# A decode block's second MLP layer with batches on partitions in four column groups, gate and residual as two VectorE operations, and one store of 32 rows

## The chip, the cores and the metric

One core of a Trainium2 chip (trn2). The metric is the device time of one execution in microseconds (us). The *span* of an execution, from its first to its last instruction, is 1.7 to 2.1 us shorter than the device time. A *landing* is the moment when the last part of a transfer has reported its arrival; the *issue* of a transfer is the instruction on SyncE or ScalarE that starts it; a *piece* is one contiguous run of bytes in it.

## The reference

A decode step of one transformer block for 8 sequences: modulation vectors from `silu(c) @ w_mod`, a layer norm, attention of 32 heads over a cache of 8192 keys and values, and an MLP. What the change touches is the last line:

```python
h = _layernorm(x) * (1 + cb) + sb
x = x + gb * (relu(h @ w1 + b1) ** 2 @ w2 + b2)     # x: 8 x 1 x 512; w1: 512 x 1792; w2: 1792 x 512
```

`gb` is a different gate for each batch and each column. Almost all the work of the kernel is elsewhere: the two caches are 268 MB.

## The kernel before

The kernel is written engine by engine with explicit semaphores: `op(engine, instruction, [what it waits for])`. A list of waits may hold both an operation and a transfer. Activations are kept transposed (128 columns of the model on the partitions, batches along the free side), so W2 is the stationary operand, 128x128 at a time, and eight batches move past it. At the end four matmuls with an identity turn the gated result back to batches on partitions, and the residual is accumulated there by four more:

```python
d_w2 = [dma("sync", s_w2[i], ...W2v[:, a:z, :]... B_w2[128*a:128*z]...)          # four pieces of W2
        for i, (a, z, j) in enumerate(((0, 4, 4), (4, 8, 4), (8, 12, 4), (12, 14, 2)))]
... # attention output, residual x1T, layer norm, first layer -> hidT (two halves, tokens k_sq[0], k_sq[1])
for f in range(FT):                                                              # FT = 14
    for k in range(KT):                                                          # KT = 4
        t = matmul(yT_ps[:, k, :], W2v[:, f, k*128:(k+1)*128], hidT[:, f, :]),   # waits [k_sq[f // 8], d_w2[f // 4]]
... # four matmuls put x1T into o_ps
k_y2 = op("vector", tensor_tensor(y2T, yT_ps, mod(5), mult), [t])
for cc in (1, 0):
    ... # two matmuls each add y2T.T to o_ps[64*cc : 64*cc+8, :]
    ... # ScalarE (cc = 1) or VectorE (cc = 0) copies these 8 rows to out_sb
    d_o.append(dma(("sync", "scalar")[cc], s_out[cc], outf[:, 256*cc:256*(cc+1)] <- out_sb[rows, :]))
Pg.wait("sync", d_o)
```

(`matmul(...)` and `tensor_tensor(...)` stand for the calls on the engine; "..." marks the rest.)

Of the kernel before, what the change touches and what calls it, by code (L numbers as in the profile page):

```python
# [5 lines left out]
ACT = mybir.ActivationFunctionType  # L6
ALU = mybir.AluOpType
AX = mybir.AxisListType
FP32 = mybir.dt.float32
BF16 = mybir.dt.bfloat16  # L10
# [23 lines left out]
class Prog:  # L34
# [19 lines left out]
    def op(self, eng, fn, deps=()):  # L54
        o = Op(eng, fn, deps, None, self.at)
        o.tok = Tok(o, self.at)
        self.ops[eng].append(o)
        return o.tok

    def dma(self, eng, sem, fn, deps=()):  # L60
        self.dma_n[sem] = self.dma_n.get(sem, 0) + 16
        self.ops[eng].append(Op(eng, fn, deps, sem, self.at))
        return Tok(None, self.at, sem, self.dma_n[sem])
# [105 lines left out]
def bass_adaLN_cond__gqa_block_cached__dense_activation_squared_relu__decode_kernel(  # L169
    nc, A_x, A_k_cache, A_v_cache, A_wq, A_wo, B_x, B_w1, B_b1, B_w2, B_b2, c, w_mod, out):  # L170
    B, _, D = A_x.shape
# [5 lines left out]
    KT = D // 128  # L177
    FT = F // 128
# [8 lines left out]
    with ExitStack() as es:  # L187
        E = es.enter_context
        sb = lambda name, shape, dt: E(nc.sbuf_tensor(name, shape, dt))
# [18 lines left out]
        IDENT = sb("IDENT", [128, 128], BF16)  # L208
# [4 lines left out]
        SEL = sb("SEL", [128, 4, 8], BF16)  # L213
# [9 lines left out]
        xT = sb("xT", [128, KT, B], BF16)  # L223
        modT = sb("modT", [128, 24, B], FP32)
        cb1 = sb("cb1", [128, KT, B], FP32)
        b_row = sb("b_row", [4, 512 + 128], BF16)
        SELB = sb("SELB", [4, 4, B], BF16)
        SELP = sb("SELP", [128, B], FP32)
        x1T = sb("x1T", [128, KT, B], BF16)
        sqs = sb("sqs", [128, B], FP32)  # L230
        std2 = sb("std2", [128, B], FP32)
        rstd2 = sb("rstd2", [128, B], FP32)
        hbT = sb("hbT", [128, KT, 2, B], BF16)

        KF = KTb[:, :, :, :].rearrange("p a t r -> p (a t r)")
        c_sb = KF[0:B, 0:512]
# [4 lines left out]
        csT = KF[:, 4096:4096 + 32 * KT].rearrange("p (k r) -> p k r", k=KT)  # L241
        haT = KF[:, 4224:4224 + 32 * KT].rearrange("p (k r) -> p k r", k=KT)
        ca1 = KF[:, 4352:4416].bitcast(FP32).rearrange("p (k b) -> p k b", k=KT)
        tmpT = KF[:, 4416:4480].bitcast(FP32).rearrange("p (k b) -> p k b", k=KT)
        EYE = KF[:, 4480:4544].bitcast(FP32).rearrange("p (g b) -> p g b", g=4)
        EYEB = KF[:, 4544:4576].rearrange("p (g b) -> p g b", g=4)
# [4 lines left out]
        sqT = KF[:, 2432:2496].bitcast(FP32).rearrange("p (k b) -> p k b", k=KT)  # L251
        hidT = KF[:, 2560:2560 + FT * B].rearrange("p (f b) -> p f b", f=FT)
        out_sb = KF[:, 2048:2304]
        oPe = KF[:, 2816:3008].rearrange("p (x j b) -> p x j b", x=6, j=4)
        oP = KF[:, 3008:3072].rearrange("p (g j b) -> p g j b", g=2, j=4)
        proj = KF[:, 4096:5120].bitcast(FP32)
        b1_row, b2_row = b_row[:, 0:512], b_row[:, 512:640]
        y2T = KF[:, 0:KT * B].rearrange("p (k b) -> p k b", k=KT)
        rT = KF[:, 1024:1024 + 2 * FT * B].bitcast(FP32).rearrange("p (f b) -> p f b", f=FT)
# [21 lines left out]
        s_last = [sem(f"d_l{i}") for i in range(3)]  # L281
        s_out = [sem(f"d_o{i}") for i in range(2)]

# [9 lines left out]
        def pool(fn, deps=()):  # L293
            return op("gpsimd", fn, deps)
# [3 lines left out]
        pool(lambda e: e.memset(ONESMB[:], 1.0 / D))  # L298
        pool(lambda e: e.memset(epst[:], EPS))
        pool(lambda e: e.memset(R4[:], 0.0))  # L300
        pool(lambda e: e.memset(Qmask[:], 1.0))
# [8 lines left out]
        def select(ap, pattern, base, cm, fill, cmp, dep):  # L310
            return pool(lambda e: e.affine_select(ap, ap, pattern=pattern, compare_op=cmp, fill=fill,
                                                  base=base, channel_multiplier=cm), [dep])
# [7 lines left out]
        t = pool(lambda e: e.memset(EYEB[:], 0.0))  # L320
        t = select(EYE[:], [[-32, 4], [-1, B]], 0, 1, 1.0, NE, t)
        t = k_eye = select(EYEB[:], [[-32, 4], [-1, B]], 0, 1, 1.0, NE, t)
        k_q0 = pool(lambda e: e.memset(QTm[:], 0.0))
# [8 lines left out]

        for i in range(4):
            for cg in range(4):
                for half in range(2):
                    t = select(SEL[:, i, 4 * half:4 * half + 4], [[-1, 4]], -(32 * cg + 8 * i + 4 * half), 1,
                               1.0, NE, t)

# [3 lines left out]
        t = select(PERM[:], [[-1, 4], [0, 4], [-4, 32]], 0, 1, 1.0, NE, t)  # L342
        t = select(SELB[:], [[-1, 4], [0, B]], 0, 1, 1.0, NE, t)
        t = pool(lambda e: e.memset(oTn[:], 0.0), [t])
# [31 lines left out]
        for k in range(KT):  # L376
            t = op("tensor", lambda e, k=k: e.matmul(csT_ps[:, k, :], cs_k[:, k, :], IDENT[0:B, 0:B],
                                                    is_transpose=True), [k_cs, k_id])
        k_csT = op("vector", lambda e: e.tensor_copy(csT[:, :, 0:B], csT_ps), [t, k_eye])

# [41 lines left out]
        t = op("vector", lambda e: e.tensor_tensor(tmpT[:], hnT_ps, ca1[:], ALU.mult), [t, k_hnT])  # L422
        k_haT = op("vector", lambda e: e.tensor_tensor(haT[:, :, 0:B], tmpT[:], mod(0), ALU.add), [t])
        for i in range(KT):
# [23 lines left out]
        k_sb = op("vector", lambda e: e.tensor_copy(hbT[:, :, 1, :], mod(3)), [k_modT])  # L448
        k_cb1 = op("vector", lambda e: e.tensor_scalar(cb1[:], mod(4), 1.0, None, ALU.add))

        stg_free = [k_modT, None, None, k_QTm]
# [64 lines left out]
        hT_ps = [bank(i)[:, 0:16 * n].rearrange("p (f a b) -> p f a b", f=n, a=2) for i, n in enumerate((8, FT - 8))]  # L516
        yT_ps = bank(2)[:, 0:KT * B].rearrange("p (k b) -> p k b", k=KT)

# [30 lines left out]
        for b in range(B):  # L549
# [76 lines left out]
            for p in range(NP):  # L626
# [47 lines left out]
                else:  # L674
# [29 lines left out]
                    for hh, (f0, n, a, z) in enumerate(((0, 4, 0, 2), (0, 4, 2, 3), (4, 2, 3, 4))):  # L704
                        for j in range(n):
                            op("tensor", lambda e, hh=min(hh, 1), f0=f0 + j, j=j, n=n, a=a, z=z: e.matmul(
                                hT_ps[hh][:, f0:f0 + 4 * (z - a - 1) + 1:4, 1, :], brow(j, n), SELB[:, a:z, :],
                                start=(f0 == 0), stop=False, skip_group_check=True), [d_bb, s_bank_free[min(hh, 1)]])
                    op("tensor", lambda e: e.matmul(
                        yT_ps, b2_row, SELB[:, :, :], start=True, stop=False, skip_group_check=True),  # L710
                        [s_bank_free[2]])
# [24 lines left out]
        t = op("vector", lambda e: e.tensor_tensor(t1T[:], attn_ps, mod(2), ALU.mult), [k_attn])  # L736
        k_x1 = op("vector", lambda e: e.tensor_tensor(x1T[:], t1T[:], xT[:], ALU.add), [t])
        mean_ps = bank(3)[:, 0:B]
# [3 lines left out]
        bc = lambda ap: ap.unsqueeze(1).to_broadcast([128, KT, B])  # L742
        t = op("vector", lambda e: e.tensor_tensor(xcT[:], x1T[:], bc(mean_ps), ALU.subtract), [t])
        k_xc = t
# [7 lines left out]
        for k in range(KT):  # L752
# [4 lines left out]
            for f in range(FT):  # L757
# [3 lines left out]
                if k == KT - 1 and f in (7, FT - 1):  # L761
# [7 lines left out]
                        hidT[:, fs, :], rT[:, fs, :], 0.0, rT[:, fs, :], ALU.max, ALU.mult), [t]))  # L769
        o_ps = bank(4)[:, 0:256]  # L770
        for f in range(FT):
            for k in range(KT):
                t = op("tensor", lambda e, f=f, k=k: e.matmul(  # L773
                    yT_ps[:, k, :], W2v[:, f, k * 128:(k + 1) * 128], hidT[:, f, :],
                    start=False, stop=(f == FT - 1), skip_group_check=True), [k_sq[f // 8], d_w2[f // 4]])
        for cc in range(2):
            for k in range(2):
                op("tensor", lambda e, k=k, cc=cc: e.matmul(
                    o_ps[64 * cc:64 * cc + B, 128 * k:128 * (k + 1)], x1T[:, 2 * cc + k, :], IDENT[:, :],
                    start=(k == 0), stop=False, tile_position=(0, 64 * cc), skip_group_check=True), [k_x1])  # L780
        k_y2 = op("vector", lambda e: e.tensor_tensor(y2T, yT_ps, mod(5), ALU.mult), [t])
        outf = out.rearrange("b s d -> (b s) d")
        d_o = []
        for cc in (1, 0):
            for k in range(2):
                t = op("tensor", lambda e, k=k, cc=cc: e.matmul(
                    o_ps[64 * cc:64 * cc + B, 128 * k:128 * (k + 1)], y2T[:, 2 * cc + k, :], IDENT[:, :],
                    start=False, stop=(k == 1), tile_position=(0, 64 * cc), skip_group_check=True), [k_y2])
            rows = slice(64 * cc, 64 * cc + B)
            if cc == 0:  # L790
                t = op("vector", lambda e, rows=rows: e.tensor_copy(out_sb[rows, :], o_ps[rows, :]), [t])
            else:
                t = op("scalar", lambda e, rows=rows: e.activation(out_sb[rows, :], o_ps[rows, :], ACT.Copy), [t])
            d_o.append(dma(("sync", "scalar")[cc], s_out[cc], lambda e, cc=cc, rows=rows: e.dma_start(
                outf[:, 256 * cc:256 * (cc + 1)], out_sb[rows, :]), [t]))
        Pg.wait("sync", d_o)

# [30 lines left out]
```

## Time and profile before

| | before |
|---|---|
| time, first three runs | 668.56 us median, 668.41 to 669.83 |
| span of the trace | 666.73 us |
| bytes read | 283.66 MB, at 425 GB/s over the span |
| last piece of W2 landed (semaphore in the trace) | 663.33 us |
| last store issued | 664.92 us |

How to read it: the kernel is a stream of bytes with computation beneath it, and only what comes behind the last landing is bare. The prediction shows the lines. I call the stretch from the last W2 landing to the end of the span *the tail*: 666.73 - 663.33 = 3.40 us. The tail, and not the device time, is the measure for this change, since the device time of one and the same kernel moves by more than a microsecond from run to run.

### The profile page before, as it was taken

To read this page: it belongs to the slowest core of one execution; us is meant where nothing else is said; L and a number is where in the kernel's file an instruction comes from. 1 tells how busy PE (TensorE), PEld (TensorE's weight loads), DVE (VectorE), ACT (ScalarE), POOL (GpSimd) and SP (SyncE) were. 2 spreads that over 40 slices of the span, in tenths; PEclk is the share of its full clock that TensorE was granted. 3 is DMA by queue.
4 is the path that set the end of the run, shared out by engine and by line. 5 is a ranking of instruction groups with operands and counts; after the bars stand their busy time and mean duration, and the time that the engine had idled before them with its cause. 6 is when DMAs were issued, how large, how long until landed. Compare 5 with 4: busy or idle time off the path is not lost.

```text
span 666.7 us, 15924 instructions
## 1 busy us (share of the span) xinstructions
PE 528.3 (79%) x7259; PEld 352.2 (53%) x7259; DVE 307.9 (46%) x587; ACT 264.3 (40%) x307; POOL 20.5 (3%) x79
## 2 busy tenths in 40 slices
PE   3494976898849987599858988499776998589887
PEld 2383732675328742477316753287424773277535
DVE  1262741466316652367415662167513673146633
ACT  2151631466115651166314661166512663146611
POOL 7400000000000000000000000000000000000000
PEclk9696998799969999699998999799997999879996
DMA  9999999999999999999999999999999999999997
GB/s 375 437 406 441 419 433 433 425 434 431 438 427 433 433 434 427 434 434 425 434 431 438 427 431 434 434 427 431 438 425 434 433 436 427 431 434 434 427 420 285
DMA packets 12189, 283.85 MB, mean 426 GB/s; under 512 B 1261, under 2 KB 1297, under 8 KB 3601
## 3 DMA queue, kind: packets, MB, share of 16 engines
q1 hardware_dynamic: 12128, 283.65, 99.3%
q8 instruction: 9, 0.15, 0.1%
q10 hardware_dynamic: 48, 0.02, 0.0%
q14 instruction: 4, 0.02, 0.0%
HBM read 283.66 MB, written 0.01 MB: 425 GB/s over the span
## 4 chain that ended last, share of the span: by engine, by line
PE 52%; DMA 38%; ACT 6%; DVE 2%; issue 1%; SPq 0%; DVEq 0%
PE PS L488 36%; DMA ring<-in_A_k_cache_dram 33%; PE PS L505 9%; ACT P_sb L582 5%; DMA ring<-in_A_v_cache_dram 4%; DMA ring<-in_A_wq_dram 2%; PE PS L636 2%; PE PS L478 1%; ACT KTb L493 1%; DVE O_sb L656 1%; PE PS L472 1%; PE PS L594 1%; DVE Pm L608 0%; PE PS L614 0%; PE PS L773 0%
## 5 line engine op out<-in xcount | busy, mean ns | idle before, releaser
L488 PE MATMUL PS<-IDENT,ring 128*128 128x128 bf16 x4096 | 267.1, 227 | 56.2 <-DMA ring<-in_A_k_cache_dram 56.2
L488 PEld LDWEIGHTS PS<-IDENT,ring 128*128 128x128 bf16 x4096 | 246.5, 102 | 104.8 <-DMA ring<-in_A_k_cache_dram 57.4
L493 ACT ACTIVATE KTb<-PS 128x1024 bf16<-128x1024 bf16 x192 | 196.5, 1024 | 236.6 <-PE PS L488 236.6
L495 DVE COPY KTb<-PS 128x1024 bf16<-128x1024 bf16 x320 | 210.0, 688 | 146.5 <-PE PS L488 144.4
L636 PE MATMUL PS<-ring,Pm 128*32 128x512 bf16 x1018 | 67.2, 409 | 24.8 <-DMA ring<-in_A_v_cache_dram 23.9
L505 PE MATMUL PS<-KTb,Qb 128*32 128x512 bf16 x1024 | 79.0, 385 | 4.5 <-ACT KTb L493 4.5
L656 DVE CAST O_sb<-PS 128x512 bf16<-128x512 f32 x31 | 21.5, 692 | 112.7 <-PE PS L636 112.7
L636 PEld LDWEIGHTS PS<-ring,Pm 128*32 128x32 bf16 x1018 | 26.5, 101 | 61.8 <-DMA ring<-in_A_v_cache_dram 33.7
L535 ACT ACTIVATE KTb<-PS 32x192 bf16<-32x192 f32 (+1 forms) x18 | 5.6, 310 | 110.0 <-PE PS L472 103.9
L582 ACT ACTIVATE P_sb<-PS,negm 128x1024 bf16<-128x1024 f32 x32 | 35.2, 1111 | 20.2 <-DVE negm L577 20.2
L478 PE MATMUL PS<-ONES 128*128 128x512 f32 x80 | 42.1, 630 | 0.0
L472 PE MATMUL PS<-IDENT 128*128 128x512 bf16 x112 | 33.4, 380 | 0.0
L594 PE MATMUL PS<-IDENT,P_sb 128*128 128x128 bf16 x256 | 19.9, 220 | 15.4 <-ACT P_sb L582 15.4
L608 DVE COPY Pm<-PS 64x512 bf16<-64x512 bf16 x48 | 20.2, 421 | 25.0 <-PE PS L594 24.5
L594 PEld LDWEIGHTS PS<-IDENT,P_sb 128*128 128x128 bf16 x256 | 14.4, 98 | 25.1 <-ACT P_sb L582 25.1
L505 PEld LDWEIGHTS PS<-KTb,Qb 128*32 128x32 bf16 x1024 | 15.4, 94 | 21.0 <-ACT KTb L493 8.5
L512 DVE TENSOR_REDUCE m<-PS 128x1 f32<-128x512 f32 x32 | 22.1, 689 | 6.6 <-PE PS L505 6.6
L660 PEld LDWEIGHTS PS<-SEL,O_sb 128*128 128x128 bf16 x124 | 5.8, 97 | 30.0 <-DVE O_sb L656 30.0
L478 PEld LDWEIGHTS PS<-ONES 128*128 128x128 f32 x80 | 12.7, 190 | 10.6 <-issue 10.6
L660 PE MATMUL PS<-SEL,O_sb 128*128 128x8 bf16 x124 | 7.8, 169 | 12.3 <-DVE O_sb L656 12.0
L472 PEld LDWEIGHTS PS<-IDENT 128*128 128x128 bf16 x112 | 9.9, 104 | 10.1 <-issue 7.2
L543 PE MATMUL PS<-wo_sb,KTb 128*32 128x512 bf16 x192 | 11.8, 380 | 3.3 <-ACT KTb L535 3.3
(134 smaller groups left out, 147.0 us busy)
## 6 DMA issues: line engine op xcount, KB each, us to landing
ring<-in_A_k_cache_dram SPq DMA_DIRECT2D x32, 4096.0 KB, 34.0
ring<-in_A_v_cache_dram SPq DMA_DIRECT2D x31, 4096.0 KB, 27.8
ring<-in_A_wq_dram SPq DMA_DIRECT2D x1, 4096.0 KB, 19.8
wo_sb<-in_A_wo_dram SPq DMA_DIRECT2D x1, 4096.0 KB, 47.3
ring<-in_w_mod_dram SPq DMA_DIRECT2D x1, 3072.0 KB, 10.5
ring<-in_A_v_cache_dram SPq DMA_DIRECT2D x1, 2048.0 KB, 22.5
ring<-in_B_w_dram SPq DMA_DIRECT2D x3, 512.0 KB, 19.2
ring<-in_B_w_dram SPq DMA_DIRECT2D x1, 1344.0 KB, 17.8
```

The lines of the kernel that those rows point to most:

```text
L472: ts = [op("tensor", lambda e: e.matmul(bank(at).rearrange("p (a r) -> p a r", a=4), IDENT[:, :], rhs)) for _ in range(n)]
L478: ts = [op("tensor", lambda e: e.matmul(bank(at).rearrange("p (a r) -> p a r", a=4), ONES[:, :], rhs)) for _ in range(n)]
L488: t = op("tensor", lambda e, j=j, i=i: e.matmul(STG[j][:, i, :], src[:, 32 * k + 8 * j + i, :], IDENT[:, :], is_transpose=True), [loaded[n ...
L493: stg_free[j] = op("scalar", lambda e, j=j, dst=dst: e.activation(dst, STG[j], ACT.Copy), [t])
L495: stg_free[j] = op("vector", lambda e, j=j, dst=dst: e.tensor_copy(dst, STG[j]), [t])
L505: t = op("tensor", lambda e, hf=hf, q=q, rhs=rhs: e.matmul(PS[32 * q:32 * (q + 1), k, :], Qb[:, 2 * p + hf, :], rhs, start=(p == 0 and hf ...
L512: return op("vector", lambda e: e.tensor_reduce(m4[:, k:k + 1], bank(k), AX.X, ALU.max), [t])
L582: exps.append(op("scalar", lambda e, k=k: e.activation(P_sb[:, k, :, :, :], bank(k).rearrange("p (i x) -> p i x", i=8).unsqueeze(2).to_bro ...
L594: t = op("tensor", lambda e, k=k, i=i: e.matmul(STG[k][:, i, :], P_sb[:, k, i, :, :].rearrange("p h x -> p (h x)"), IDENT[:, :], is_transp ...
L608: done.append(op("vector", lambda e, dst=dst, frm=frm: e.tensor_copy(dst, frm), [t, k_pm]))
L636: t = op("tensor", lambda e, m=m, cg=cg, p=p, vt=vt, Obank=Obank: e.matmul(Obank[32 * cg:32 * (cg + 1), :], lhs[:, p, 32 * m:32 * m + 32], ...
L656: t = op("vector", lambda e, osb=osb, Obank=Obank: e.tensor_copy(osb, Obank), [t])
```

## The change

The intent: make the activations the stationary operand, so that the second layer's result comes out with batches on partitions straight away. The four blocks of 128 output columns go to four column groups of the PE array (output partitions 32k to 32k+31). The closing transposes and copies fall away; gate and residual become two VectorE operations of 128x128, and one store writes 32 rows of 256 B. A column group is 32 wide and there are eight batches, so the activations are padded: batch b sits in column 4b, with zeros between. The output row of batch b in block k is then on partition 32k + 4b, that is on every fourth partition. The core of the diff:

```diff
-        SELB = sb("SELB", [4, 4, B], BF16)
+        SELB = sb("SELB", [4, 4, 32], BF16)
-        x1T = sb("x1T", [128, KT, B], BF16)
+        x1w = sb("x1w", [128, KT, B, 4], BF16)
+        hidw = sb("hidw", [128, FT, B, 4], BF16)
+        mod5 = sb("mod5", [128, 128], FP32)
+        x1T, hidT = x1w[:, :, :, 0], hidw[:, :, :, 0]
...
-        (32 small GpSimd selects that fill SEL)
+        for cg in range(4):
+            t = select(SEL[:], [[-8, 4], [-1, 8]], -32 * cg, 1, 1.0, NE, t)
...
+        for k in range(KT):          # the gate, as rows
+            op("vector", lambda e, k=k: e.tensor_copy(
+                mod5[32 * k:32 * (k + 1), :], mod_r[96:128, 1, 128 * k:128 * (k + 1)]), [k_mr1])
...
+            if f == F2:              # F2 = 12: in front of the last two of 14
+                for k in range(KT):
+                    k_res = matmul(x1_ps[32*k:32*(k+1), :], x1w[:, k], IDENT, tile_position=(0, 32*k))
             for k in range(KT):
-                matmul(yT_ps[:, k, :], W2v[:, f, k*128:(k+1)*128], hidT[:, f, :])
+                matmul(y_ps[32*k:32*(k+1), :], hidw[:, f], W2v[:, f, k*128:(k+1)*128], tile_position=(0, 32*k))
-        (four residual and four transposing matmuls, gate, two copies, two stores)
+        t = op("vector", lambda e: e.tensor_tensor(y_sb, y_ps, mod5[:], ALU.mult), [t])
+        t = op("vector", lambda e: e.tensor_tensor(out_sb, y_sb, x1_ps, ALU.add), [t, k_res])
+        d_o = dma("sync", s_out, lambda e: e.dma_start(
+            bass.AP(out.tensor, out.offset, [[128, KT], [D, B], [1, 128]]), out_sb[0:128:4, :]), [t])
```

(Long calls shortened to `matmul(...)`, parts in parentheses told in words, cuts marked "...".)

More of the change, by code (lines that the diff above doesn't have):

```diff
@@ L251, in bass_adaLN_cond__gqa_block_cached__dense_activation_squared_relu__decode_kernel @@
         sqT = KF[:, 2432:2496].bitcast(FP32).rearrange("p (k b) -> p k b", k=KT)
-        hidT = KF[:, 2560:2560 + FT * B].rearrange("p (f b) -> p f b", f=FT)
-        out_sb = KF[:, 2048:2304]
+        out_sb = KF[:, 2048:2176]
+        y_sb = KF[:, 5120:5376].bitcast(FP32)
         oPe = KF[:, 2816:3008].rearrange("p (x j b) -> p x j b", x=6, j=4)
@@ L257, in bass_adaLN_cond__gqa_block_cached__dense_activation_squared_relu__decode_kernel @@
         b1_row, b2_row = b_row[:, 0:512], b_row[:, 512:640]
-        y2T = KF[:, 0:KT * B].rearrange("p (k b) -> p k b", k=KT)
         rT = KF[:, 1024:1024 + 2 * FT * B].bitcast(FP32).rearrange("p (f b) -> p f b", f=FT)
@@ L281, in bass_adaLN_cond__gqa_block_cached__dense_activation_squared_relu__decode_kernel @@
         s_last = [sem(f"d_l{i}") for i in range(3)]
-        s_out = [sem(f"d_o{i}") for i in range(2)]
+        s_out = sem("d_o")
         d_c = dma("scalar", s_c, lambda e: e.dma_start(c_sb, c))
@@ L299, in bass_adaLN_cond__gqa_block_cached__dense_activation_squared_relu__decode_kernel @@
         pool(lambda e: e.memset(epst[:], EPS))
+        pool(lambda e: e.memset(x1w[:], 0.0))
+        pool(lambda e: e.memset(hidw[:], 0.0))
         pool(lambda e: e.memset(R4[:], 0.0))
@@ L320, in bass_adaLN_cond__gqa_block_cached__dense_activation_squared_relu__decode_kernel @@
         t = pool(lambda e: e.memset(EYEB[:], 0.0))
-        t = select(EYE[:], [[-32, 4], [-1, B]], 0, 1, 1.0, NE, t)
-        t = k_eye = select(EYEB[:], [[-32, 4], [-1, B]], 0, 1, 1.0, NE, t)
+        t = select(EYE[:], [[-32, 4], [-4, B]], 0, 1, 1.0, NE, t)
+        t = k_eye = select(EYEB[:], [[-32, 4], [-4, B]], 0, 1, 1.0, NE, t)
         k_q0 = pool(lambda e: e.memset(QTm[:], 0.0))
@@ L331, in bass_adaLN_cond__gqa_block_cached__dense_activation_squared_relu__decode_kernel @@
             t = select(R4m[:], [[-1, 32]], -d, 1, 0.5, NE, t)
-        for i in range(4):
-            for cg in range(4):
-                for half in range(2):
-                    t = select(SEL[:, i, 4 * half:4 * half + 4], [[-1, 4]], -(32 * cg + 8 * i + 4 * half), 1,
-                               1.0, NE, t)
+        for cg in range(4):
+            t = select(SEL[:], [[-8, 4], [-1, 8]], -32 * cg, 1, 1.0, NE, t)
         t = pool(lambda e: e.memset(SELP[:], 0.0), [t])
@@ L342, in bass_adaLN_cond__gqa_block_cached__dense_activation_squared_relu__decode_kernel @@
         t = select(PERM[:], [[-1, 4], [0, 4], [-4, 32]], 0, 1, 1.0, NE, t)
-        t = select(SELB[:], [[-1, 4], [0, B]], 0, 1, 1.0, NE, t)
+        t = select(SELB[:], [[-1, 4], [0, 32]], 0, 1, 1.0, NE, t)
         t = pool(lambda e: e.memset(oTn[:], 0.0), [t])
@@ L378, in bass_adaLN_cond__gqa_block_cached__dense_activation_squared_relu__decode_kernel @@
                                                     is_transpose=True), [k_cs, k_id])
-        k_csT = op("vector", lambda e: e.tensor_copy(csT[:, :, 0:B], csT_ps), [t, k_eye])
+        k_csT = op("vector", lambda e: e.tensor_copy(csT[:, :, 0:32:4], csT_ps), [t, k_eye])
         xT_ps = bankb(5)[:, 0:KT * B].rearrange("p (k b) -> p k b", k=KT)
@@ L422, in bass_adaLN_cond__gqa_block_cached__dense_activation_squared_relu__decode_kernel @@
         t = op("vector", lambda e: e.tensor_tensor(tmpT[:], hnT_ps, ca1[:], ALU.mult), [t, k_hnT])
-        k_haT = op("vector", lambda e: e.tensor_tensor(haT[:, :, 0:B], tmpT[:], mod(0), ALU.add), [t])
+        k_haT = op("vector", lambda e: e.tensor_tensor(haT[:, :, 0:32:4], tmpT[:], mod(0), ALU.add), [t])
         for i in range(KT):
@@ L516, in bass_adaLN_cond__gqa_block_cached__dense_activation_squared_relu__decode_kernel @@
         hT_ps = [bank(i)[:, 0:16 * n].rearrange("p (f a b) -> p f a b", f=n, a=2) for i, n in enumerate((8, FT - 8))]
-        yT_ps = bank(2)[:, 0:KT * B].rearrange("p (k b) -> p k b", k=KT)
+        y_ps = bank(2)[:, 0:128]
         def permute(pP, q0, q1, dst, deps, fill, then=None):
@@ L706, in bass_adaLN_cond__gqa_block_cached__dense_activation_squared_relu__decode_kernel @@
                             op("tensor", lambda e, hh=min(hh, 1), f0=f0 + j, j=j, n=n, a=a, z=z: e.matmul(
-                                hT_ps[hh][:, f0:f0 + 4 * (z - a - 1) + 1:4, 1, :], brow(j, n), SELB[:, a:z, :],
+                                hT_ps[hh][:, f0:f0 + 4 * (z - a - 1) + 1:4, 1, :], brow(j, n), SELB[:, a:z, 0:B],
                                 start=(f0 == 0), stop=False, skip_group_check=True), [d_bb, s_bank_free[min(hh, 1)]])
                     op("tensor", lambda e: e.matmul(
-                        yT_ps, b2_row, SELB[:, :, :], start=True, stop=False, skip_group_check=True),
+                        y_ps, SELB[:, :, :].rearrange("o a r -> o (a r)"), b2_row, start=True, stop=False, skip_group_check=True),
                         [s_bank_free[2]])
@@ L736, in bass_adaLN_cond__gqa_block_cached__dense_activation_squared_relu__decode_kernel @@
         t = op("vector", lambda e: e.tensor_tensor(t1T[:], attn_ps, mod(2), ALU.mult), [k_attn])
-        k_x1 = op("vector", lambda e: e.tensor_tensor(x1T[:], t1T[:], xT[:], ALU.add), [t])
+        k_x1 = op("vector", lambda e: e.tensor_tensor(x1T, t1T[:], xT[:], ALU.add), [t])
         mean_ps = bank(3)[:, 0:B]
@@ L742, in bass_adaLN_cond__gqa_block_cached__dense_activation_squared_relu__decode_kernel @@
         bc = lambda ap: ap.unsqueeze(1).to_broadcast([128, KT, B])
-        t = op("vector", lambda e: e.tensor_tensor(xcT[:], x1T[:], bc(mean_ps), ALU.subtract), [t])
+        t = op("vector", lambda e: e.tensor_tensor(xcT[:], x1T, bc(mean_ps), ALU.subtract), [t])
         k_xc = t
@@ L769, in bass_adaLN_cond__gqa_block_cached__dense_activation_squared_relu__decode_kernel @@
                         hidT[:, fs, :], rT[:, fs, :], 0.0, rT[:, fs, :], ALU.max, ALU.mult), [t]))
-        o_ps = bank(4)[:, 0:256]
+        x1_ps = bank(4)[:, 0:128]
         for f in range(FT):
+            if f == F2:
+                for k in range(KT):
+                    k_res = op("tensor", lambda e, k=k: e.matmul(
+                        x1_ps[32 * k:32 * (k + 1), :], x1w[:, k].rearrange("p b r -> p (b r)"), IDENT[:, :],
+                        tile_position=(0, 32 * k)), [k_x1])
             for k in range(KT):
@@ L773, in bass_adaLN_cond__gqa_block_cached__dense_activation_squared_relu__decode_kernel @@
                 t = op("tensor", lambda e, f=f, k=k: e.matmul(
-                    yT_ps[:, k, :], W2v[:, f, k * 128:(k + 1) * 128], hidT[:, f, :],
-                    start=False, stop=(f == FT - 1), skip_group_check=True), [k_sq[f // 8], d_w2[f // 4]])
-        for cc in range(2):
-            for k in range(2):
-                op("tensor", lambda e, k=k, cc=cc: e.matmul(
-                    o_ps[64 * cc:64 * cc + B, 128 * k:128 * (k + 1)], x1T[:, 2 * cc + k, :], IDENT[:, :],
-                    start=(k == 0), stop=False, tile_position=(0, 64 * cc), skip_group_check=True), [k_x1])
@@ L781, in bass_adaLN_cond__gqa_block_cached__dense_activation_squared_relu__decode_kernel @@
-        k_y2 = op("vector", lambda e: e.tensor_tensor(y2T, yT_ps, mod(5), ALU.mult), [t])
-        outf = out.rearrange("b s d -> (b s) d")
-        d_o = []
-        for cc in (1, 0):
-            for k in range(2):
-                t = op("tensor", lambda e, k=k, cc=cc: e.matmul(
-                    o_ps[64 * cc:64 * cc + B, 128 * k:128 * (k + 1)], y2T[:, 2 * cc + k, :], IDENT[:, :],
-                    start=False, stop=(k == 1), tile_position=(0, 64 * cc), skip_group_check=True), [k_y2])
-            rows = slice(64 * cc, 64 * cc + B)
-            if cc == 0:
-                t = op("vector", lambda e, rows=rows: e.tensor_copy(out_sb[rows, :], o_ps[rows, :]), [t])
-            else:
-                t = op("scalar", lambda e, rows=rows: e.activation(out_sb[rows, :], o_ps[rows, :], ACT.Copy), [t])
-            d_o.append(dma(("sync", "scalar")[cc], s_out[cc], lambda e, cc=cc, rows=rows: e.dma_start(
-                outf[:, 256 * cc:256 * (cc + 1)], out_sb[rows, :]), [t]))
@@ L796, in bass_adaLN_cond__gqa_block_cached__dense_activation_squared_relu__decode_kernel @@
-        Pg.wait("sync", d_o)
+                    y_ps[32 * k:32 * (k + 1), :], hidw[:, f].rearrange("p b r -> p (b r)"), W2v[:, f, k * 128:(k + 1) * 128],
+                    start=False, stop=(f == FT - 1), tile_position=(0, 32 * k), skip_group_check=True),
+                    [k_sq[f // 8], d_w2[f // 4]])
+        t = op("vector", lambda e: e.tensor_tensor(y_sb, y_ps, mod5[:], ALU.mult), [t])
+        t = op("vector", lambda e: e.tensor_tensor(out_sb, y_sb, x1_ps, ALU.add), [t, k_res])
+        d_o = dma("sync", s_out, lambda e: e.dma_start(
+            bass.AP(out.tensor, out.offset, [[128, KT], [D, B], [1, 128]]), out_sb[0:128:4, :]), [t])
@@ L798, in bass_adaLN_cond__gqa_block_cached__dense_activation_squared_relu__decode_kernel @@
+        Pg.wait("sync", [d_o])
         with nc.Block("blk") as block:
```

## The prediction

> **What bounds the kernel now.** I read the page first, for which resource is full; then the end of the run in finer and finer windows, because the diff touches almost only that. The page:
>
> ```profile
> span 666.7 us, 15924 instructions
> ...
> PEclk9696998799969999699998999799997999879996
> DMA  9999999999999999999999999999999999999997
> ...
> HBM read 283.66 MB, written 0.01 MB: 425 GB/s over the span
> ```
>
> Read the DMA row: every slice is at 90% or more except the last. The kernel streams 283.66 MB and nothing else sets the pace for some 660 us. PE at 79% and VectorE at 46% are averages over work hidden beneath that stream. A change that moves no bytes can win only in front of the first transfer or behind the last one. So the next view is by stretches at the end (columns: stretch, length, busy time of PE, PE weight load, VectorE, ScalarE, GpSimd, granted clock, DMA share, GB/s):
>
> ```profile
> 660.00:661.00 1.00, 0.68 (x16) 0.58 (x15) 0.32 (x2) 0.27 (x1) 0.00 (x0) 0.50 1.00 393
> 661.00:662.00 1.00, 0.32 (x12) 0.32 (x13) 0.88 (x5) 0.00 (x0) 0.00 (x0) 0.50 0.67 264
> 662.00:663.00 1.00, 0.87 (x34) 0.81 (x31) 0.21 (x1) 0.00 (x0) 0.00 (x0) 0.50 0.27 92
> 663.00:664.00 1.00, 1.00 (x27) 0.70 (x24) 0.19 (x1) 0.00 (x0) 0.00 (x0) 0.50 0.00 0
> ```
>
> The stream is full until 661 and dry shortly before 663. What it brings last is W2, the second layer's weights. The view of the line that loads W2 in four pieces:
>
> ```profile
> L682 SPq DMA_DIRECT2D ring<-in_B_w_dram x4: 885/1444/5533, 641.0 to 649.9; - x4
> ...
> DMA to landing us min/median/max: 13.5/17.0/19.2
> ```
>
> The last piece is issued at 649.9 and lands after 13.5 us, the shortest of the four: about 663.4. Now the timeline of the last stretch (start, length, engine, line, and in brackets the idle time before it):
>
> ```profile
> 661.68 0.93 PEld L773 LDWEIGHTS PS<-KTb,ring 128*128 128x128 bf16 x32 [1.09 <-DVE KTb L768]
> ...
> 662.80 0.86 PEld L773 LDWEIGHTS PS<-KTb,ring 128*128 128x128 bf16 x24 [0.19 <-issue]
> ...
> 663.78 0.19 DVE L781 TENSOR_TENSOR KTb<-PS,modT 128x32 bf16<-128x32 f32 x1 [1.56 <-PE PS L773]
> ...
> 664.03 0.38 PE L786 MATMUL PS<-IDENT,KTb 128*8 128x128 bf16 x4
> 664.44 0.37 ACT L793 ACTIVATE KTb<-PS 8x256 bf16<-8x256 f32 x1 [3.90 <-PE PS L786]
> 664.49 0.41 DVE L791 CAST KTb<-PS 8x256 bf16<-8x256 f32 x1 [0.51 <-PE PS L786]
> 664.85 0.30 ACTq L794 DMA_DIRECT2D out_dram<-KTb  x1
> 664.92 0.31 SPq L794 DMA_DIRECT2D out_dram<-KTb  x1
> ```
>
> and, from the same view of a narrower stretch:
>
> ```profile
> 663.37 0.37 PE L773 MATMUL PS<-KTb,ring 128*128 128x8 bf16 x8
> ```
>
> The trap is here. The second layer looks like 56 matmuls from 661.68 to 663.74, that is 2.06 us of PE work on the path. But its activations were ready for the second half at 662.22 (the last operation on L768 starts at 662.01 and takes 0.21), and the matmuls stop after 32, with an idle labelled "issue", and resume at 662.80. The view names no releaser; the third W2 piece must be. The last eight start at 663.37, which is the landing of the fourth piece. I therefore take the last eight as released by a transfer, not by the matmuls before them: 0.37 us of PE work is on the path, not 2.06.
>
> **What the Trainium skill says.** "TensorEngine Tiling (Array Packing)", section Performance Considerations, recommends just this swap: where the moving side is 32 columns or fewer, make it stationary and use four column tiles. Its section Tiling Modes says that the tiles run in parallel. The trace agrees: the attention values (L636) with 32-column weights and 512 moving columns take 1.91 us for 32, or 60 ns each, while one alone lasts 379 ns. "TensorE: Matmul & The Clock Gate", Part 1, describes a cold state at half clock after an idle stretch; the trace shows the granted clock at 0.50 in all of the last rows above. "VectorE: DVE Perf Modes", section The perf-mode tier table, gives tensor_tensor with an operand in PSUM no speed-up. The trace agrees: 128x32 takes 0.19 us, 128x64 0.23, and a 128x512 cast 0.69, so about 1.04 ns a column upon 0.16. "DMA: Bandwidth & Descriptors", Specifications, says that transfers under 512 B are not at line rate; no run so far shows what 256 B costs here.
>
> **The change, part by part.**
>
> *Second layer.* 56 pairs before and 56 after, now 32-column weights and 128 moving columns in four groups. At half clock the earlier projections (L402, the same shape but 512 columns) take 3.60 us for 32, or 112 ns each, so 128 columns are about 28 ns each: 56 x 28 = 1.6 us against 56 x 36.8 (2.06/56) = 2.06. That gain of 0.5 us is **hidden**, since W2 lands when it lands. Of the last eight, two rounds of four groups, I expect 0.38 to 0.42 us: the four matmuls of L786 are two rounds of two groups with 128 columns at this clock, and take 0.38. So about the same as the 0.37 now: 0 to +0.05. The 16 of the third piece and the four residual matmuls, which the instruction order puts just before the last eight, need about 20 x 28 = 0.56 us from 662.80, that is until 663.36. They just fit in front of 663.37.
>
> *Behind the last matmul, removed.* From 663.74 to the store's issue at 664.92 stand the gate (0.19), the four transposing matmuls (0.38), the copies (0.41) and the hand-overs between engines: 1.18 us.
>
> *Added.* Two tensor_tensor of 128x128 in a row on one engine: 0.16 + 128 x 1.04 = 0.29 us each. As a check, the copy of 128x128 from PSUM (L427) takes 292 ns. A hand-over of 0.04 before, 0.03 between (as between L764 and L766), 0.02 behind: 0.67 us. **Path: 1.18 - 0.67 = 0.51 us less.**
>
> *Store.* One of 32 pieces of 256 B on one queue, for two of eight pieces of 512 B on two. The wait view has SyncE waiting 1.0 us for the store behind an issue of 0.31: 664.92 to 666.28, almost all fixed. The bytes are the same 8 KB. One final wait instead of two saves perhaps 0.05; more and smaller pieces may cost 0.05 to 0.15. Net 0 to +0.1.
>
> *Front.* GpSimd drops 28 of its 32 selects of the table SEL, at about 0.33 us from start to start (29 take 9.48): some 9 us, and adds two memsets (0.6). VectorE adds four 32x128 copies, about 1 us, before the loop, where it now idles 2.9 us until GpSimd is done at 29.4. But the first key transposes wait for their transfer until 30.84, and the DMA row is full there. Worth 0.
>
> *Strided activations* (one column of four) touch small VectorE operations in front of W2's landing, which have about half a microsecond of room: 0.
>
> Sum: -0.51 (path) + 0.02 (last eight) + 0.05 (store) = about **-0.45 us**, or 0.07%.
>
> **Rivals.** (1) The full PE gain counts: if the wait at 662.80 were issue only and not W2, a further 0.5 us or so would go and the time would be near 667.6. For it: the view's word "issue". Against: two stops at the boundaries of W2's pieces, and the landing at 663.4. (2) The store takes back the gain: if pieces of 256 B to HBM cost several tenths, the time stays at 668.5. For it: the skill's threshold. Against: the span of such a small store is nearly all latency. (3) The column groups fall behind the landing: if loading padded weights were slower than 28 ns a pair, the 20 matmuls before the last piece would end after 663.37 and push everything; at 40 ns a pair that is 0.25 us, and the time is near 668.4. (4) The stream itself ends earlier or later, since instruction fetches and code placement differ: a few tenths either way, and no part of the change's intent.
>
> **Range and chances.** 668.56 - 0.45 = 668.1. The three runs before spread from 668.41 to 669.83, so a median can sit a few tenths high; the rivals span 667.6 to 668.5. I take 667.6 to 668.7 for 8 in 10. A change of 2% would be 13 us; everything behind 661 is 6 us, so a gain of 2% is all but impossible, and a loss needs a stall that the instruction order gives no place for.
>
> **What would show it.** Right: the last eight second-layer matmuls still start at about 663.4, released by W2; the two VectorE operations take about 0.29 us each; the store is issued about 0.5 us earlier; SyncE still waits about 1.0 us for it; GpSimd ends near 21 us without moving the first transposes. Wrong: the matmuls end before 663 (rival 1), the wait for the store grows by 0.3 or more (rival 2), no stop stands before the last eight (rival 3), or the last W2 piece lands at another time (rival 4).

## The result, and the profile after

| | before | after |
|---|---|---|
| time, first comparison | 669.09 us median of 4 (668.41 to 669.83) | 668.71 us median of 4 (668.28 to 668.77) |
| ratio | | 0.9993, 95% interval 0.9975 to 1.001 |
| ratio, five more rounds (`again_after`) | | 0.9999, 0.9987 to 1.0011 |
| span, in two traces each | 666.73, 666.58 | 666.87, 666.92 |
| last W2 landing | 663.33, 663.17 | 663.53, 663.57 |
| tail | 3.40, 3.41 | 3.34, 3.34 |

A ratio is the mean time of one kernel's fast runs over that of the other's fast runs of the same rounds, so it is not quite the ratio of the medians. Neither ratio differs from one. The tail does: it repeats to within 0.01 us and is 0.06 us shorter. That is what the change is worth inside the span, where 0.45 was predicted.

Outside the span it loses. Device time less span is 1.78 us on average in the kernel before (40 fast runs) and 1.93 us in the changed kernel (10 fast runs; spans to 0.1 us). The difference goes with the store: 1.93 us in `plain_wrong` below, which also stores from SyncE alone, and 1.76 and 1.79 us in `rows_adjacent_four` and `store_two_queues`, which store from SyncE and ScalarE as the kernel before does. Why is not known. With this 0.15 us added to the tail, the change comes out about 0.1 us slower than before. That is an estimate, and the ratios can't tell it from zero.

The end of the timeline after the change answers to the lines shown of before (columns: start, length, engine, line, operation, shapes, and the idle time before it):

```profile
662.22 0.28 DVE L772 SCALAR_TENSOR_TENSOR hidw<-KTb 128x48 bf16<-128x48 f32 x1
663.00 0.38 PEld L782 LDWEIGHTS PS<-ring,hidw 128*32 128x32 bf16 x16 [0.27 <-issue]
...
663.57 0.40 PE L782 MATMUL PS<-ring,hidw 128*32 128x128 bf16 x8
664.03 0.29 DVE L786 TENSOR_TENSOR KTb<-PS,mod 128x128 f32<-128x128 f32 x1 [1.53 <-PE PS L782]
664.35 0.29 DVE L787 TENSOR_TENSOR KTb<-KTb,PS 128x128 bf16<-128x128 f32 x1
664.67 0.66 SPq L788 DMA_DIRECT2D out_dram<-KTb  x1
```

Three things are to be seen. The stop in front of the third W2 piece is still there, at 663.00, though its activations were ready at 662.50; the piece itself landed at 662.89 (before: resumed at 662.80, activations 662.22, landing 662.69). The last eight matmuls start at 663.57, just behind the landing at 663.53. So the second layer waits for W2 as before. The two VectorE operations take 0.29 us each. And the store's issue on SyncE takes 0.66 us, where each of the two stores before took 0.31 and 0.30. Cut at the landing and at the last store's issue, by the trace's times (the store on SyncE in both; differences are taken before rounding):

| stretch | before | after | difference |
|---|---|---|---|
| last W2 landing to the gate operation | 0.46 | 0.50 | +0.05 |
| gate operation to the (last) store's issue | 1.14 | 0.64 | -0.50 |
| issue on SyncE | 0.31 | 0.66 | +0.35 |
| end of the issue to its first data packet | 0.50 | 0.63 | +0.13 |
| first data packet to the last landing of the store | 0.54 | 0.50 | -0.03 |
| last landing to the end of the span | 0.46 | 0.40 | -0.06 |
| tail | 3.40 | 3.34 | -0.06 |

The expected half microsecond was won between the engines and given back in the store. The issue alone gives back 0.35. The wait view of SyncE shows less of this than one would think, since it begins only where the issue ends; before, then after:

```profile
SPq L116 <- DMA out_dram<-KTb: 1.0, 1, 1.0
```

```profile
SPq L792 <- DMA out_dram<-KTb: 1.1, 1, 1.1
```

Whoever looks only at how long the end waits for the store sees 0.1 us more and misses the larger part.

### The profile page after: what moved, and what is told of

It is laid out like the page before. It is cut to its first block, busy times and chain, and to the rows that moved or that the text cites. A ratio compares the mean times of both kernels' runs of the same rounds, so it can differ in the third digit from the quotient of the medians.

```text
span 666.9 us, 15863 instructions
## 1 busy us (share of the span) xinstructions
PE 526.9 (79%) x7255; PEld 353.1 (53%) x7255; DVE 309.8 (46%) x591; ACT 263.9 (40%) x306; POOL 16.1 (2%) x53
## 4 chain that ended last, share of the span: by engine, by line
PE 52%; DMA 38%; ACT 6%; DVE 2%; issue 1%; SPq 0%; DVEq 0%
PE PS L492 37%; DMA ring<-in_A_k_cache_dram 32%; PE PS L509 9%; ACT P_sb L586 5%; DMA ring<-in_A_v_cache_dram 4%; DMA ring<-in_A_wq_dram 2%; PE PS L640 2%; PE PS L482 1%; ACT KTb L497 1%; DVE O_sb L660 1%; PE PS L476 1%; PE PS L598 1%; DVE Pm L612 0%; PE PS L618 0%; PE PS L782 0%
## 5 line engine op out<-in xcount | busy, mean ns | idle before, releaser
L640 PE MATMUL PS<-ring,Pm 128*32 128x512 bf16 x1018 | 64.1, 394 | 23.2 <-DMA ring<-in_A_v_cache_dram 22.3
```

The source lines that it names most:

```text
L640: t = op("tensor", lambda e, m=m, cg=cg, p=p, vt=vt, Obank=Obank: e.matmul(Obank[32 * cg:32 * (cg + 1), :], lhs[:, p, 32 * m:32 * m + 32], ...
```

## The experiments

Two questions were open. **Why is the store dear?** By theory A the number of its pieces (32 for 8), by B the blocks of its address pattern (4 blocks of 8 rows), by C its pieces being under 512 B or the partition step of four. **And did the column groups save PE time** that W2's landing hid, as the prediction said, or none at all?

### The form of the store, five at a time (`store_forms`)

```diff
-        d_o = dma("sync", s_out, <the store>, [t])
+        for fn in forms:                       # five stores, the last one the right one
+            d_o = dma("sync", s_out, fn, [t, d_o])
```

> The changed kernel with five stores one after the other on SyncE, each waiting for the one before; the last is the right one, so the output is correct. Forms in order: 8 pieces of 512 B; 8 of 256 B; 16 of 256 B (2 blocks of 8 rows); 32 of 256 B as one list of 32 rows; 32 of 256 B as 4 blocks of 8 rows (the changed kernel's). Theory A (the issue costs by the number of pieces): 0.31, 0.31, about 0.43, 0.66, 0.66 us. Theory B (it costs by the number of blocks in the address pattern): 0.31, 0.31, 0.43, 0.31, 0.66. Theory C (pieces under 512 B or the partition stride of four are what is slow): the second is already well over 0.31. If it is chance of the one profile, all lie near 0.31.

SyncE's timeline; each store waits for the one before, so each issue stands alone:

```profile
664.28 0.32 SPq L790 DMA_DIRECT2D out_dram<-KTb  x1
665.53 0.76 SPq L791 DMA_DIRECT2D out_dram<-KTb  x1
667.34 0.57 SPq L792 DMA_DIRECT2D out_dram<-KTb  x1
669.01 0.52 SPq L793 DMA_DIRECT2D out_dram<-KTb  x1
670.73 0.57 SPq L794 DMA_DIRECT2D out_dram<-KTb  x1
```

The third form, 16 pieces in two blocks, took 0.57 as well. Eight pieces cost more (0.76) than 32 (0.57), so A is out; one list of 32 rows is hardly cheaper than four blocks of eight (0.52), so B does not explain it alone. What the dear ones share against the first is the piece size and the partition step. Those two had to be taken apart.

### Piece size against partition step (`store_forms2`, `store_forms3`)

The same loop with other forms; neighbouring partitions are written `W[0:8, 0:128]`, every fourth `W[0:32:4, 0:128]`.

> The changed kernel with five stores in a row, the last the right one. In order: 8 pieces of 256 B from neighbouring partitions; 8 of 512 B from every fourth partition; 8 of 512 B from neighbouring partitions (the control, 0.32 us before); 32 of 256 B from neighbouring partitions; the changed kernel's own. Theory P (the source's partition step of four makes the issue dear): 0.32, over 0.5, 0.32, about 0.35, 0.57. Theory S (pieces of 256 B make it dear): over 0.5, 0.32, 0.32, over 0.5, 0.57. Theory O (only the place in the row counts, the first is cheap): only the first is at 0.32.

```profile
664.29 0.32 SPq L791 DMA_DIRECT2D out_dram<-KTb  x1
665.49 0.77 SPq L792 DMA_DIRECT2D out_dram<-KTb  x1
667.32 0.30 SPq L793 DMA_DIRECT2D out_dram<-KTb  x1
668.55 0.32 SPq L794 DMA_DIRECT2D out_dram<-KTb  x1
669.90 0.59 SPq L795 DMA_DIRECT2D out_dram<-KTb  x1
```

> As store_forms2 with other forms: 16 of 512 B from every fourth partition; 16 of 512 B from neighbouring ones; 16 of 256 B from neighbouring ones; 8 of 256 B from every fourth; the changed kernel's own. Theory P: over 0.5, 0.32, 0.32, over 0.5, 0.57. Theory S: 0.32, 0.32, over 0.5, over 0.5, 0.57. Theory O: the first cheap, the others not.

In its order: 0.61, 0.35, 0.33, 0.71 and 0.58 us. Both runs came out as theory P (the partition step) had it, piece by piece. Small pieces cost nothing: 8 of 256 B from neighbouring partitions landed 1.19 us after their issue began, 8 of 512 B after 1.21, and 32 of 256 B after 1.33. I took P for settled here. The next runs showed that it was only half of it.

### Other partition steps (`store_forms4`)

> Five stores in a row as in store_forms, for which partition steps are dear: 8 pieces of 256 B from every second partition; 8 from every eighth; 8 from every sixteenth; 32 from every second; the changed kernel's own (every fourth, 0.57 to 0.60). If every step other than one is dear, all take 0.5 to 0.8; if the issue grows with the range of partitions spanned, 8 pieces at step two are near 0.4 and at step sixteen over 0.8.

8 pieces at step two: 0.77; at step eight: 0.59; at step sixteen: 0.56; 32 pieces at step two: 0.49; the changed kernel's own: 0.57. Every step other than one is dear, and it does not grow with the range of partitions; rather the reverse.

### The change's store with the step alone undone (`adjacent_wrong`)

```diff
-            bass.AP(out.tensor, out.offset, [[128, KT], [D, B], [1, 128]]), out_sb[0:128:4, :]), [t])
+            bass.AP(out.tensor, out.offset, [[128, KT], [D, B], [1, 128]]), out_sb[0:32, :]), [t])
```

> The changed kernel with its one store reading 32 neighbouring partitions in place of every fourth one, to the same 4 blocks of 8 rows of the output; nothing else differs. The output is wrong on purpose. If the partition step is the cause, the issue takes 0.32 us in place of 0.66, the last landing comes 1.33 us after the issue starts in place of 1.80, and the stretch behind W2's last landing is 2.9 us in place of 3.34. If the blocks of the output pattern are what is dear, the issue stays at 0.6.

Its output is wrong, which doesn't matter for the time. The expectation of P failed:

```profile
664.41 0.77 SPq L788 DMA_DIRECT2D out_dram<-KTb  x1
```

The issue took 0.77 us, more than the changed kernel's 0.66, and the tail was 3.46. So the step is not needed for a dear store: four blocks of eight rows at the destination are enough, even from neighbouring partitions. (This rests on one trace.)

### Neither step nor blocks (`plain_wrong`)

```diff
-            bass.AP(out.tensor, out.offset, [[128, KT], [D, B], [1, 128]]), out_sb[0:128:4, :]), [t])
+            bass.AP(out.tensor, out.offset, [[128, 32], [1, 128]]), out_sb[0:32, :]), [t])
```

> The changed kernel with its one store of 32 pieces of 256 B in the plainest form: 32 neighbouring partitions to 32 rows behind one another (wrong output on purpose). It differs from adjacent_wrong only in the output pattern, one list of 32 rows in place of 4 blocks of 8. If either a partition step or a block pattern is enough to make the issue dear, here neither is there: issue 0.32 us, last landing 1.33 us after it starts, 2.9 us from W2's last landing to the end (3.34 in the changed kernel, 3.40 before), which is what the prediction's sum asked for. If the issue stays at 0.6 or more behind the tail of this kernel, something else than the form of the store makes it dear. Time against before 0.9993, the noise about 0.001.

Again wrong: the bytes go to the wrong places, but they are as many, in as many pieces.

```profile
663.97 0.29 DVE L787 TENSOR_TENSOR KTb<-KTb,PS 128x128 bf16<-128x128 f32 x1
664.28 0.35 SPq L788 DMA_DIRECT2D out_dram<-KTb  x1
```

The issue took 0.35 us, the last landing came 1.37 us after it began, and the tail was 2.91 us, as expected: 0.43 less than the changed kernel and 0.49 less than the kernel before. Everything else in the kernel is the change's, so this is the sum of the prediction with a store as cheap as the prediction took it to be. Of the 0.49 some 0.15 are lost again outside the span (above), so by estimate 0.34 is left. The device time does not show even that: 668.26 us median of 6 against 668.37 of 11, ratio 1.0001 (0.9989 to 1.0013). The noise of a run is larger than half a microsecond.

### Two ways to a cheaper store with the right output

Half of the store on each of two queues (`store_two_queues`):

```diff
+        d_o = [dma(e, s_out[h], lambda e, h=h: e.dma_start(
+            bass.AP(out.tensor, out.offset + 256 * h, [[128, 2], [D, B], [1, 128]]), out_sb[64 * h:64 * h + 64:4, :]), [t])
+            for h, e in enumerate(("sync", "scalar"))]
```

> The changed kernel with its store cut in two halves of 16 pieces of 256 B, one on SyncE and one on ScalarE. If the issue cost is by pieces or by blocks, each issue takes about 0.43 us in place of 0.66 and the end comes 0.2 to 0.3 us earlier, counted from the landing of the last W2 piece (3.35 us now, 3.05 to 3.15 expected). If the small pieces themselves are slow in landing, the issue shrinks but the wait behind it stays and less than 0.1 us is won. Time against before: below the noise of a run, 0.999.

A miss: the issues took 0.65 and 0.64 us side by side, so half the pieces are not half the cost; the first data packet of ScalarE's half came 0.27 us behind that of SyncE's; the last landing came 2.00 us after the first issue, and the tail was 3.60. The time, 669.25 us median of 4 against 668.34 of 7 (ratio 1.0011, 0.9994 to 1.0028), is not told from one either. In this trace W2's last piece landed only at 664.44, of which more below.

Batches on neighbouring partitions and four stores in the plain form (`rows_adjacent_four`):

```diff
-        x1w = sb("x1w", [128, KT, B, 4], BF16)      # hidw likewise
+        x1w = sb("x1w", [128, KT, 4, B], BF16)
-        x1T, hidT = x1w[:, :, :, 0], hidw[:, :, :, 0]
+        x1T, hidT = x1w[:, :, 0, :], hidw[:, :, 0, :]
+        d_o = [dma(e, s_out[k % 2], lambda e, k=k: e.dma_start(
+            outf[:, 128 * k:128 * (k + 1)], out_sb[32 * k:32 * k + B, :]), [t])
+            for k, e in enumerate(("sync", "scalar", "sync", "scalar"))]
```

> A right version: the eight batches of a column group on eight neighbouring partitions (the zero columns of the padded activations stand behind them, not between), stored by four stores of 8 pieces of 256 B, two one after the other on each of SyncE and ScalarE. Each issue 0.32 us, so the second of a queue starts 0.33 us after the first, and lands 1.2 us after its own start: 1.5 us from the first issue in place of 1.80, plus 0.06 for a second wait. The stretch behind W2's last landing 3.1 us against 3.34 (changed) and 3.40 (before). The time: 0.3 us under before, 0.9995, inside the noise. If the landing and not the issue is what grew, nothing is won: 3.3 or more.

The output is right. Each issue is cheap, 0.30 to 0.32 us, so the padding's order is a free choice that makes the store plain. But there are two on a queue (a line for each queue, both stores merged):

```profile
664.47 0.66 SPq L789 DMA_DIRECT2D out_dram<-KTb  x2
664.48 0.67 ACTq L789 DMA_DIRECT2D out_dram<-KTb  x2
```

and the last landing came 1.78 us after the first issue, not 1.5: the second store of a queue took 1.43 us from its own issue, where a lone one of this form took 1.19 in `store_forms2`. The tail was 3.38. Time: 668.46 us median of 6 against 668.45 of 11, ratio 0.9997 (0.9984 to 1.001). No right version that I ran beats the changed kernel's tail. With the time outside the span added, `rows_adjacent_four` would be ahead of the changed kernel by 0.13 us and of the kernel before by 0.04, by estimate (3.38 + 1.76 against 3.34 + 1.93 and 3.40 + 1.78), but none is told from the kernel before by its time. A right version with one plain store would need the 32 rows on neighbouring partitions in the order of the output. The column groups set their results 32 partitions apart, and I did not find a cheap way.

### What the column groups do to PE time (`w2_first_old`, `w2_first_new`)

```diff
-   d_w1 = [... the two pieces of W1 ..., [released[s0]]];  d_w2 = [... the four pieces of W2 ...]
+   d_w2 = [... the four pieces of W2 ..., [released[s0]]];  d_w1 = [... the two pieces of W1 ...]
```

With W2 loaded first it has landed by 659.05 in the one and 659.03 in the other, and the second layer waits only for its activations. That bares its PE time, in the kernel before and in the changed one.

> The kernel before, with W2 loaded ahead of W1, so that the second layer no longer waits for a transfer but only for its activations. Its 56 pairs should then run from the first activations on without the two stops, at about 27 ns a pair (1.5 us), the time some 2 us longer than before since the first layer's last quarter now comes behind the last landing.

> The changed kernel with W2 loaded ahead of W1. Theory of the prediction (column groups save about 0.5 us of PE time, hidden by W2's landing): the second layer from its first matmul to its last result is about 0.4 to 0.5 us shorter than in w2_first_old. Rival (at half clock a column-group matmul takes 107/4 = 27 ns, the same as a pair of the kernel before, so there is nothing to hide): equal pace, and 0.1 to 0.3 us longer for the four residual matmuls and the longer last matmul.

The kernel before, W2 first:

```profile
665.90 1.66 PE L773 MATMUL PS<-KTb,ring 128*128 128x8 bf16 x56 [1.00 <-DVE KTb L768]
```

```profile
667.60 0.19 DVE L781 TENSOR_TENSOR KTb<-PS,modT 128x32 bf16<-128x32 f32 x1 [1.15 <-PE PS L773]
```

The changed kernel, W2 first:

```profile
665.94 1.47 PE L782 MATMUL PS<-ring,hidw 128*32 128x128 bf16 x48 [1.07 <-DVE KTb L768]
...
667.20 0.32 PE L778 MATMUL PS<-IDENT,x1w 128*32 128x128 bf16 x4
...
667.30 0.43 PE L782 MATMUL PS<-ring,hidw 128*32 128x128 bf16 x8
667.78 0.29 DVE L786 TENSOR_TENSOR KTb<-PS,mod 128x128 f32<-128x128 f32 x1 [1.30 <-PE PS L782]
```

From the first second-layer matmul to the gate: 667.60 - 665.90 = 1.70 us before, 667.78 - 665.94 = 1.84 us after. The rival was right: there was no PE gain for W2 to hide, but a small loss. At the granted clock of 0.5 a pair of the kernel before starts every 27 ns, and the column groups start four matmuls every 107 ns, which is 27 ns each. The 0.14 us more are the four residual matmuls, one round of 0.11 us, and a last matmul that lasts longer (0.31 us against 0.17), less about 0.12 us because the four matmuls of a round start together, so that the last one starts earlier. Without the residual round the two would be nearly equal. These two ran once each (672.27 and 672.62 us); only their traces are used.

### The same kernels again (`again_after`, `again_before`)

> The changed kernel unchanged, for the time against before in five rounds and for a second trace. From the traces the stretch behind the landing of the last W2 piece is 3.41 us before and 3.34 us after, so the true difference should be within 0.2 us and not be told from zero: ratio 0.999 to 1.001. If the prediction's sum holds, 0.9993 with the same stretch 0.45 us shorter. W2's last landing may lie anywhere from 663.1 to 664.5.

> The kernel before unchanged, for a second trace: the stretch from the last W2 landing to the end stays 3.4 us within 0.1; the landing itself may move by some tenths, as it does between traces of the changed kernel.

The ratio of `again_after`, 0.9999, stands in the table above (668.69 us median of 6 against 668.48 of 11); `again_before` took 668.40 us in its one run. The tails repeated: 3.34 and 3.41. The landing moves by itself: `after`, `adjacent_wrong` and `plain_wrong` differ in no instruction in front of the store, and their last W2 piece landed at 663.53, 663.27 and 663.14. So the 0.2 us by which it came later in the changed kernel's first trace cannot be laid to the change. In `store_two_queues` fifteen of the sixteen parts of that piece had landed by 663.06 and the last one at 664.44. Such a straggler would explain executions a microsecond longer than the rest, of which the kernel before has its share (668.23 to 670.13 us in one set of 11), but I did not trace enough of them to say so.

## Why the prediction was right or wrong

The time held as far as can be told: no ratio differs from one, and 668.71 us lies at the upper edge of the stated range (668.7). That is no evidence for its sum: the range also holds the 668.56 us of the kernel before from which it set out. The medians of the first comparison differ by 0.38 us, close to the 0.45 predicted, but that is luck: in the five further rounds they differ by 0.21 the other way. The mechanism promised 0.45 us in the tail and gave 0.06. By its own steps:

- **What bounds the kernel, and the last eight matmuls as the start of the path: right.** They still start 0.04 us behind the landing of the last W2 piece, in both kernels and in every trace in which W2 comes last. Calling the idle "issue" a wait for W2, rival 1's reverse, was right: with W2 loaded early the 56 run through without a stop.
- **The last eight, "0 to +0.05": right.** Landing to gate grew by 0.05 us. The 16 and the four residual matmuls fitted in front, as worked out.
- **The path behind them, "-0.51": right.** It measured -0.50, and the two operations took 0.29 us each, as computed from the rows of the kernel before.
- **The store, "net 0 to +0.1": the term that was mis-sized.** From the last issue to the end it took 2.20 us in place of 1.80, so +0.39. Rival 2 named the place but the wrong cause: pieces of 256 B are not dear here. The prediction used the issue's 0.31 us as though every store had it. It holds for the plain form only, and the change left that form twice over, with its partition step and its blocks. `plain_wrong` puts the plain form back and recovers the missing 0.43 us. The prediction's own sign for rival 2, a wait for the store that grows by 0.3 us or more, would have missed it: the wait grew by 0.1 and the issue by 0.35. The final wait that fell away did save about what was forecast, 0.06 us for 0.05, but the 0.15 us outside the span were not foreseen.
- **PE gain "hidden", 1.6 us against 2.06: wrong, though without effect on the sum.** The 36.8 ns a pair were 2.06 / 56 over a stretch that the prediction itself had just found to contain two waits for W2. Without the waits it is 27 ns, the same as for the column groups. A mean over a stretch with stops in it is no pace.
- **Strided activations, "0": right.** The two writes of L772 took 0.30 and 0.28 us where the kernel before took 0.23 and 0.21, and were done 0.39 us before the third piece of W2 landed.
- **The check that column tiles run in parallel: right, by the wrong comparison.** That one matmul lasts 379 ns says little, since consecutive matmuls overlap. Untiled 512-column matmuls (L472, granted clock 1.00) start 216 ns apart; those of L636 start four at a time, 216 ns apart.
- **Front, "worth 0": consistent.** GpSimd was done at 20.97 us as forecast (near 21), and the first key transposes still waited for their transfer, to 31.02 us in place of 30.84. No run undoes this part alone, so it is read from the trace and not tested.
- **Rival 4 (the stream ends at another time): it moves more than the whole effect.** A few tenths, and once more than a microsecond.

What stays open: why a step or a block makes the issue dear, and why eight pieces at step two or four (0.71 to 0.77 us) were dearer than 32 (0.49 to 0.60, and 0.66 where the changed kernel's store stands alone). The runs show that each of the two is enough, not how. One trait is common to every dear store of SyncE in the traces: its first data packet comes 0.63 to 0.65 us after the end of the issue, that of a cheap one 0.46 to 0.50 us after it where no other store of its queue is under way. Two things were not separated. A store in four blocks has 4 packets of 4 B beside its data and a list of 32 rows has 16, so blocks and the spread over queues go together here; yet the stepped list with 16 such packets took 0.52 us, so the spread alone doesn't set the cost. And `plain_wrong` writes 32 rows behind one another; 32 evenly spaced rows with gaps between them were not tried, only 8.

## What to carry to other kernels

A layout that saves work between engines also fixes the form of the transfer behind it: when it puts rows on stepped partitions or in blocks, measure the issue itself on the issuing engine, and not only the wait behind it. Before dividing a stretch by its count of instructions, take out the stretches in which they waited. And where the time of a run is noisier than the effect, measure from the event that bounds the path to the end of the trace: here that repeated to 0.01 us while the time could not tell half a microsecond. Then check that the device time outside the span stayed the same; here it grew by 0.15 us.

## What the Trainium skill lacked or had wrong

- "DMA: Bandwidth & Descriptors", section Issuing engines are not separate DMA queues, says that the issuing sequencer's time is usually small beside the transfer. For this store of 8 KB it was 0.66 us of the 1.80 from the start of the issue to the last landing, and no page that I read gives a cost to a partition step in the source or to blocks at the destination: 0.30 to 0.35 us from neighbouring partitions to one list of rows, whether 8, 16 or 32 pieces; 0.49 to 0.77 us with a partition step (2, 4, 8 or 16) or with blocks at the destination.
- The same page, section Specifications, sets 512 B as the least size for line rate. For a store that is nearly all latency that is no guide: 8 pieces of 256 B landed 1.19 us after the start of the issue, 8 of 512 B after 1.21 us.
- "TensorEngine Tiling (Array Packing)", section Performance Considerations, offers the swap with four column tiles for a moving side of 32 columns or fewer, without a word on the clock. It gives every matmul a fixed overhead, but does not weigh the swapped form against the unswapped one by it. With 8 batches, 128-column blocks and a granted clock of 0.5, both forms run at 27 ns a matmul, and the swapped layer took 1.84 us in place of 1.70 to its gate.
